# A new order of steps, two row tables on other engines, a split last output chunk and paired ReLUs in a fused attention and FFT-mixing kernel

## The chip, the cores and the metric

The kernel runs on one core of a Trainium2 chip. The core has TensorE (PE in the profile; its weight loads are PEld), VectorE (DVE), ScalarE (ACT), GpSimd (POOL) and SyncE (SP). Each engine takes its instructions in the order in which they were written and waits for others by semaphores. SyncE issues most stores and all transposing transfers here, GpSimd most loads, ScalarE two small ones. The metric is the device time of one execution in microseconds (us), as the median over runs.

## The reference

```python
def phi(x):                                   # x: q or k, (8, 8, 576, 64); w_phi: (64, 128)
    proj = np.einsum('bhsd,df->bhsf', x, w_phi)
    proj = proj - np.max(np.abs(proj), axis=-1, keepdims=True)
    return np.concatenate([np.exp(proj), np.exp(-proj)], axis=-1)
q_p, k_p = phi(q), phi(k)
kv = np.einsum('bhsf,bhsd->bhfd', k_p, v)
z = np.sum(k_p, axis=2)
num = np.einsum('bhsf,bhfd->bhsd', q_p, kv)
den = np.einsum('bhsf,bhf->bhs', q_p, z)[..., None] + 1e-06
x = num / den                                 # heads side by side: (8, 576, 512)

u = x + np.real(fft(fft(x, axis=1), axis=2))  # along the 576 rows, then the 512 columns
un = (u - mean(u)) / sqrt(var(u) + 1e-06)     # over the 512 columns
out = u + np.maximum(un @ w_ch1, 0.0) @ w_ch2 # w_ch1: (512, 2048), w_ch2: (2048, 512)
```

Everything is float32 outside. There are eight batches.

## The kernel before

The work of one batch is cut into streams, each a Python generator, and each `yield` ends a step. A string, `PLAN`, has one letter for each step; `step(name)` runs the next step of that letter's stream, and a stream that has finished goes on with the next batch. So the letters' order is the order in which the instructions of all engines are written, and nothing reorders them later. A step is named here by letter, batch and number, counted from 0: F1.16 is step 16 of the forward stream of batch 1. A place in the plan is counted from 1. The string has 1236 letters before the change.

The streams of one batch:

- K, V, Q load keys, values and queries through GpSimd's queue (L289), cast to bfloat16. B and A transpose the keys and the queries by DMA through SyncE's queue (L413 to L427). The buffers of staged and transposed data are single: the loads of the next batch wait for the transposes of this one.
- T makes the features: step 0 for the last 64 key rows, steps 1 to 8 in pairs for the keys (eight matmuls to `psk`, then two exponentials of 1024 columns, L502), steps 9 to 17 for the queries (L602, L611). R takes the maxima of the keys on VectorE (L511, L516). S scales the values by exponentials of these maxima: small exponentials on ScalarE (L452, L466), multiplications on GpSimd (L456 for the last rows in S.0, L471 for a pair of heads in each of S.1 to S.4). P takes the maxima of the queries (matmuls to `psq`, L560 on VectorE); its last step, P.6, weighs them (a matmul to `pt`).
- M has 26 steps: 0 to 7 build a head's key-value matrix (`kv`, ten matmuls, a copy by ScalarE, L900), 8 to 15 combine it with the queries (L992 on TensorE, L999, L1004 and L1006 on VectorE, L1007 on GpSimd into `X`, with `cb` in two buffers), 16 to 20 are the DFT along the rows, 21 to 25 the DFT along the columns with the additions to `X` (L1099). D, between M.15 and M.16, folds rows and columns of `X` on VectorE (L908 to L932).
- N normalises: for each of five chunks of rows, statistics on VectorE (L1179, L1180), the shift on ScalarE (`UN`, L1155), a transposing DMA from SyncE to `UT` (L1172). The chunks come in the order 0, 2, 1, 3, 4. Batch 0 transposes on TensorE instead. U takes the row scales.
- F, with 68 steps, is the FFN: `hidden(0, 256)` is 16 steps of four matmuls of 256 columns into `psf` (L1224) and one ReLU (L1228) each; then output chunks 0 and 2 (8 steps of two matmuls of 512 columns into `pso` each, L1235, then an addition on VectorE and a store, L1241); `hidden(256, 576)` is 16 steps of 320 columns; then output chunks 1 and 3 and the last chunk of 64 rows (16 matmuls on half the array's columns in turn, L1260; two additions, L1267; a store of 63 rows, L1213, and one of one row, L1214). In batch 0 both hidden parts come first, so the second weight matrix is read from F0.32 on.

`psf`, `pso`, `pu` and, in the first two batches, `psq` share three PSUM banks (`pb`); `psk`, `psh`, `psD` and the combines share `pj`, two buffers of two banks; `kv`, `pt` and the small key tile share one bank (`pk`).

At the start, batch 0's raw inputs are loaded in float32 by SyncE and transposed on TensorE (G for keys, J for queries, copied out by L378 on ScalarE or L380 on VectorE). C builds the tables of angles for the DFT: `at` for rows (three blocks of 320 columns, VectorE), its absolute value `t3` (L220), `tc2` for columns (512, GpSimd), its absolute value `tc3` (L225, VectorE). H takes their sines on ScalarE (L243 to L254). Z clears paddings on GpSimd, Y keeps TensorE busy with matmuls that nothing reads (L1313), and W loads the two weight matrices through GpSimd's queue (L91, L93).

In the plan F steps of one batch stand among the steps that prepare the next ones. From F7.0 (place 1165) only four other steps follow, and the last 47 letters are all F.

## Time and profile before

| | |
|---|---|
| median of 13 runs | 437.08 us (435.97 to 439.26) |
| the profiled execution's own time | 437.75 us |
| its span (first to last instruction) | 436.0 us |
| mean granted TensorE clock | 0.993 |
| TensorE, VectorE, ScalarE, GpSimd busy | 406.2, 334.4, 308.9, 208.6 us |
| first FFN matmul of batch 0 (F0.0) | 54.3 us |
| W1b load, W2b load, issue to landing | 18.2, 15.5 us |
| median landing of a key load of 512 KB | 7.5 us |
| ReLU of 256 and of 320 columns, mean | 388, 444 ns (128 of each) |
| L178 (VectorE, 320 columns), L197 | 1.83 us and 1.91 us for three each |
| L183, L220 (VectorE, 960 columns) | 0.66 us each |
| L225 (VectorE, 512 columns) | 1.65 us |

Times inside the execution are counted from the start of the span. Busy time of TensorE is no measure of how well it is used: its matmuls are pipelined, and a matmul's span holds the time in the pipe. A line of the stretches' view has the stretch, then length, then busy time and number of instructions of PE, PEld, DVE, ACT and POOL, then the granted clock, the mean share of the DMA engines and GB/s. A line of the chain of waits has start, duration, and what the end of the program waited for at that time. A timeline's line has start, duration, engine, line, operation and tiles; SPq is the issuing of transfers by SyncE.

### The profile page before, as it was taken

How to read it: one execution, taken by the hardware profiler on the slowest of the kernel's cores; microseconds unless marked ns; L12 is line 12 of the kernel's file. 1: busy time of each engine (PE TensorE's matmuls, PEld its weight loads, DVE VectorE, ACT ScalarE, POOL GpSimd, SP SyncE). 2: the span in 40 equal slices, each digit the busy share in tenths (PEclk: the TensorE clock that was granted, in tenths of full speed). 3: DMA queues.
4: the chain of work that ended last, by engine and by line, in shares of the span. 5: the costliest groups of instructions: out<-in, count | busy, mean ns of one | idle time of the engine just before them, and what ended most of it. 6: DMA issues, size and time to landing. Idle time of an engine off the chain costs nothing.

```text
span 436.0 us, 10447 instructions
## 1 busy us (share of the span) xinstructions
PE 406.2 (93%) x4110; PEld 255.5 (59%) x4110; DVE 334.4 (77%) x685; ACT 308.9 (71%) x685; POOL 208.6 (48%) x269
## 2 busy tenths in 40 slices
PE   8888798989899999999999899999999999999993
PEld 3565466644675658565766458565766467656551
DVE  6979776799959984998679985898799875965202
ACT  2896899735994798499847798589948885355340
POOL 7982478646645093636645445823642543300100
PEclk9899999999999999999999999999999999999998
DMA  8899994986569366494898446793853150104304
GB/s 218 160 204 150 151 143 50 179 95 100 97 68 144 56 98 118 84 152 58 128 97 120 51 90 101 105 143 63 129 95 51 20 104 20 26 0 86 58 21 84
DMA packets 108626, 42.70 MB, mean 98 GB/s; under 512 B 82849, under 2 KB 103457, under 8 KB 108577
## 3 DMA queue, kind: packets, MB, share of 16 engines
q0 software_dynamic: 45936, 16.60, 35.1%
q1 hardware_dynamic: 62481, 25.38, 30.7%
q8 instruction: 32, 0.52, 0.5%
q14 instruction: 17, 0.14, 0.1%
q10 hardware_dynamic: 160, 0.07, 0.1%
HBM read 36.77 MB, written 9.44 MB: 106 GB/s over the span
## 4 chain that ended last, share of the span: by engine, by line
PE 46%; DVE 34%; ACT 12%; DMA 2%; issue 2%; POOL 2%; DVEq 0%; ACTq 0%; POOLq 0%; SPq 0%
PE psf L1224 17%; PE pso L1235 12%; DVE cb L1004 5%; DVE tg L999 4%; DVE MK L516 4%; DVE R L908 4%; PE kv L892 2%; PE pso L1260 2%; DMA UT<-UN 2%; DVE MQ L560 2%; DVE rd L1006 2%; DVE CEO L1039 2%; ACT HT L1228 2%; DVE X L1241 2%; PE psD L1050 2%
## 5 line engine op out<-in xcount | busy, mean ns | idle before, releaser
L1224 PE MATMUL psf<-UT,W1b 128*128 128x320 bf16 (+1 forms) x1024 | 142.1, 286 | 3.5 <-DMA UT<-UN 2.3
L1235 PE MATMUL pso<-W2b,HT 128*128 128x512 bf16 x512 | 125.7, 379 | 0.0
L1228 ACT ACTIVATE HT<-psf 128x256 bf16<-128x256 f32 (+1 forms) x256 | 100.0, 416 | 34.8 <-PE psf L1224 27.5
L1224 PEld LDWEIGHTS <-W1b 128*128 128x128 bf16 x1024 | 94.6, 98 | 34.9 <-issue 7.5
L1235 PEld LDWEIGHTS <-HT 128*128 128x128 bf16 x512 | 45.8, 98 | 43.9 <-issue 1.3
L1007 POOL TENSOR_TENSOR X<-cb,rd 128x320 f32<-128x320 f32 x56 | 41.1, 734 | 62.0 <-DVE rd L1006 47.3
L471 POOL TENSOR_TENSOR VCn<-VS,VCn 128x512 bf16<-128x512 bf16 x28 | 29.8, 1063 | 35.5 <-ACT VCn L466 29.6
L502 ACT ACTIVATE KPp<-psk 128x1024 bf16<-128x1024 f32 x28 | 28.8, 1029 | 22.3 <-PE psk L496 22.2
L560 DVE TENSOR_REDUCE MQ<-psq 128x8 f32<-128x1024 f32 (+1 forms) x32 | 34.2, 1083 | 10.5 <-PE psq L552 10.4
L1241 DVE SCALAR_TENSOR_TENSOR X<-pso,rs,X 128x512 f32<-128x512 f32 x32 | 23.7, 740 | 23.3 <-PE pso L1235 23.1
L502 ACT ACTIVATE KPn<-psk 128x1024 bf16<-128x1024 f32 x28 | 28.6, 1021 | 13.9 <-DVE MK L516 13.8
L516 DVE TENSOR_REDUCE MK<-psk 128x8 f32<-128x1024 f32 x28 | 34.0, 1213 | 0.3
L1099 DVE TENSOR_TENSOR X<-pu,X 128x512 f32<-128x512 f32 (+3 forms) x49 | 23.5, 528 | 11.8 <-PE pu L1109 11.7
L456 POOL TENSOR_TENSOR V4N<-VS,V4N 64x256 bf16<-64x256 bf16 x14 | 8.9, 637 | 49.0 <-ACT V4N L452 27.6
L1155 ACT ACTIVATE UN<-X,MV 128x512 bf16<-128x512 f32 (+1 forms) x35 | 25.0, 724 | 7.8 <-DVE MV L1180 4.1
L611 ACT ACTIVATE QPHP<-psh 128x1024 bf16<-128x1024 f32 x28 | 28.8, 1027 | 2.2 <-PE psh L602 2.0
L471 POOL TENSOR_TENSOR VCp<-VS,VCp 128x512 bf16<-128x512 bf16 x28 | 29.7, 1060 | 0.0
L611 ACT ACTIVATE QPHN<-psh 128x1024 bf16<-128x1024 f32 x28 | 28.8, 1027 | 0.0
L1179 DVE BATCH_NORM_STATS2 st<-X 128x6 f32<-128x512 f32 (+1 forms) x40 | 26.9, 673 | 0.0
L1195 POOL TENSOR_TENSOR rs<-VE,mhalf 128x5 f32<-128x5 f32 (+1 forms) x9 | 10.3, 1139 | 31.5 <-DVE VE L1194 31.5
L992 PEld LDWEIGHTS <-QPHP 128*128 128x128 bf16 x280 | 20.9, 99 | 5.3 <-DVE cb L1004 1.9
L289 POOL DMA_DIRECT2D QS<-in_q_dram x28 | 23.1, 827 | 0.0
(459 smaller groups left out, 800.1 us busy)
## 6 DMA issues: line engine op xcount, KB each, us to landing
out_dram<-X SPq DMA_DIRECT2D x16, 256.0 KB
out_dram<-X SPq DMA_DIRECT2D x64, 64.0 KB
KS<-in_k_dram POOLq DMA_DIRECT2D x7, 512.0 KB, 7.5
QS<-in_q_dram POOLq DMA_DIRECT2D x14, 256.0 KB, 8.1
VS<-in_v_dram POOLq DMA_DIRECT2D x14, 256.0 KB, 6.3
W1b<-in_moe_w_ch_dram POOLq DMA_DIRECT2D x1, 2048.0 KB, 18.2
W2b<-in_moe_w_ch_dram POOLq DMA_DIRECT2D x1, 2048.0 KB, 15.5
W2b<-in_k_dram SPq DMA_DIRECT2D x2, 512.0 KB
```

Of the source, the lines that this page charges most:

```text
L471: nc.gpsimd.tensor_tensor(out=VC[:, hs, :, 0:D], in0=values[b][0][:, hs, :].rearrange("p h (j d) -> p h j d", d=D), in1=VC[:, hs, :, D:D + ...
L502: nc.scalar.activation(out=KP[:, hs, :, :].rearrange("p e (jp jj) f -> p jj (e jp) f", jj=2), in_=psk[:], func=AT.Exp, scale=sgn,)
L516: nc.vector.tensor_reduce(out=MK[:, 2 * pr:2 * pr + 2, :].rearrange("p e (jp jj) -> p jj (e jp)", jj=2), in_=tiles[pr][:], axis=AX.X, op=A ...
L560: nc.vector.tensor_reduce(out=o, in_=i[:], axis=AX.X, op=ALU.max, apply_absolute_value=True)
L611: nc.scalar.activation(out=o, in_=psh[:], func=AT.Exp, scale=sgn)
L1007: nc.gpsimd.tensor_tensor(out=X[:, :, D * h:D * h + D], in0=cb[:, :, 0:D], in1=rd[:].to_broadcast([128, 5, D]), op=ALU.mult,)
L1155: nc.scalar.activation(out=UN[0:M, c, :], in_=X[0:M, c, 0:C], func=AT.Identity, scale=-1.0, bias=mv[0:M, c, 0:1],)
L1179: nc.vector.bn_stats(out=st[0:M, :], in_=X[0:M, c, 0:C])
L1224: nc.tensor.matmul(ps[:], lhsT=W1b[:, cc, 128 * hh:128 * hh + 128], rhs=UT[:, cc, lo:hi], start=(cc == 0), stop=(cc == NCC - 1),)
L1228: nc.scalar.activation(out=HT[:, hh, lo:hi], in_=ps[:], func=AT.Relu, scale=-1.0)
L1235: nc.tensor.matmul(po[:], lhsT=HT[:, hh, at:at + 128], rhs=W2b[:, hh, :], start=(hh == 0), stop=(hh == NHH - 1),)
L1241: nc.vector.scalar_tensor_tensor(out=U[:, c, 0:C], in0=po[:], scalar=scale_of[b, c], in1=U[:, c, 0:C], op0=ALU.mult, op1=ALU.add,)
```

## The change

- `PLAN` is a new string of 1239 letters. Stream C has six steps and not three. Kinds and numbers of all other steps stay.
- The row angles: the product by the row number moves to ScalarE (three activations with a per-partition scale), the count of whole turns to GpSimd (three operations) and ScalarE (one activation of 960 columns that takes `MAGIC` off), and one VectorE operation of 960 columns joins them. The column angles: the product moves to ScalarE, the rest stays on GpSimd. `magic` is a new constant.
- The last output chunk of batch 7 is computed in two halves of 256 columns, each with its own PSUM tile, additions and stores. The first half's stores go to ScalarE's queue; of the second half the 63 rows go to SyncE's and the one row to ScalarE's.
- In `hidden(0, 256)` two steps share one PSUM tile of 512 columns, and one ReLU takes both after the second.

```diff
--- before.py
+++ after.py
@@ -21,19 +21,19 @@
 
 
 PLAN = (
-    "CYCYZYYZYGTGZKGRTZGTZSGTJKJJRPTTJQRPQYWTSRTSJPTYTMMRTSMMPSTPTPTMMTTMZTPMVMQMTMVVTMDTMBHMDYYDHADYYMHY"
-    "HYMTHMMHMTRWMTNMTSMNYNTMNYNRFFRFNFSFCNFFUTMFNTUNPMFKVFRFQSMTPFTFNTFRSFQSMUFKUVBFTUFMPTPPMTUKFFTQMPFT"
-    "FMTPTFMMTFFFUMFMFATMRKFFFMVFTQDFRTMFFFFFFFMFMFFPTFDFFDSFRFQTFFTMDFFFTFFMFFFFMRFFTFFSMSFMFRPSTMYMTTNF"
-    "QFPTNPPFSMMTMMTMPTMFBFFMTFMFFKFMNFFMFTPFVFFMTNFNUMAFFMTMFFFVMRFTFRFFMFTFFFVMFKFMFMFFTFPFFFRDFTFFDFTP"
-    "FFFFDFDFFQRMTMPFFFFFFMTFSFSMRFMFTFTMTQFNFFTSTMMNFMBSFPPMMFTFFMPTMTFFSFMTQFPFFFMFFMNFFFMTFVMNMFFMFMNF"
-    "UFMFFFMFAFFMTFMFKVFTFFFRFRFMFTFFVQKTPFRFFFDTFFFTDFFFDQFFFDRMFFTMTFSFFMFSMRFFTFMFTPFMFFSTTMNFFNMFFTFT"
-    "NFMFFFMMSTPMSFTQFMFFPPTBMFFFMNKFMNFFMFVTPFMFFPUMFFMFAMFFMTFRFMFFMFFFVMTFRFKFTFMFVFFFQDQTPFFFFRFDTFFT"
-    "PFFFDDFFFRMTFFFTFFFMSMMFSRFTMFTFTMFMTFTNNMFMFMFMTFSFMTPSMFTNFFFPPPSFFMFFFFBMFFMTFFMFVFPTQFFMNNUMAFVF"
-    "FMFTMFKTFRFFRSFFMTFFFFMMKFFFTVFMFFQFRPFTQFDFFMTRFDFFFFFFFDFTDFFMFFFMTFMFSMFMFFRTTMFTMFFTNFTNFSMFTMMM"
-    "TFNSFPMFTFSFMPQFFMFTPPBMFFMTPFFMFPNFFVMAFNUMMFFTFMFMFFMFFFFTRVPFRFTFFFMFFFMFTVFFRMFFDDFTFFFTPFFFFFDF"
-    "FDFRTMTFMFFFFMMFSSFMRFTFMTFTTFMNFFFNSMTFMMSFMFTTFTNFFPMFSFPPTFMFFFMFFFMFNPMFFMFFPNFFFMMFFFTUMMFFFFFM"
-    "FMFFFMFMFFFFMFFDDFFFFFFDFFDFMMFFFFMFFMMFFFMFMNNFMFFFFFFFFNFFMFFFFFFFFFFFFFFFMFFNFNFFFFFFUFFFFFFFFFFF"
-    "FFFFFFFFFFFFFFFFFFFFFFFFFFFFFFFFFFFF"
+    "YYCCYCYGCGZTGRTGZTZTZRZJQQGSTJRKTPYTSTPRYTWJJJRMPTMTSSMTPPSTPTMTZQMTMMTMPMMVKBTCMTMDTYMVHMYYDYYDDAHM"
+    "HYYHTHMMMHKMTTRMNMTMYQNNYVMSNTKNMFFNFNRRFSTPFTPTUFWMNFFMNFFSFRTFVMFFTCURPSYUBNTUTFSUFMFQKTFMFTPPMQTP"
+    "VMTFFPUTFUMTMFFAFMMTFFMQFMFDFRFMFTVFFFFRFMFTFFMFFPFFTFFFQDDFFFRFMFTKFFDMTFFFFTFMFFMFRTFMRTFMFSSSSTTM"
+    "NPFFTNPBTMMMSMQFTMTPPMFFMFFTMFFFPVTAMFFFPNFFMTFFMNNKUMFFVMMFFQTMFFTFRMRFFTFFFQFMFFMFMFFFPTFFRFFFFDFD"
+    "VFTPFFFDFFDKTPRFTFFMMTSFFBFFFMMSSFFMFFRTMTMFFTNMSMFFFTNPPMFMTFFFTMTFSTPMFFFMFFQPFTFMFFVFNMFFFMKTFFAM"
+    "NNMFFMFUMFVFFMVQFFMFTTRFFMFFFKFRFFMTQFFFDTMRFFFFFDTPFFFTDDFRPFFFFFMTFTFMFFMFBMRFSSMFFTTTMFMTFFFTFNFN"
+    "SFMTTMMFFFPMFTMSTPPMFFSMTFFMNFPFMFFPFFVKMNQKFFMNMUFFMFFMFFVMFAFMFQMFFMFTTRFQRFFFTVFMFFFFDFTPFRFFFPDT"
+    "FFFTFFFDFFFDRTMTMFFFFMBFSMFFSMRFTFTTMSFMFTFNMMMTMFTFFFMNFPSSTMTNFFFFTPPMFFFMFTFPQMFVFKFPFFMFFMANMFFN"
+    "FFMKFFMFTUTFMFFRFRFFSVFMFFFFFTMFTFQFRMFDVTFFFMTRFFDFFFFFFFDFFDFTMFTBQFMFFMSFMFRFMFTFTTMFFSMTNFTNFFMP"
+    "SMFFMMTFMPTFSMTFFMTPFMFTFFQMFNPPPFVMFFAMFFPFNNUMVFMFTFMFMFFFMFRFFMTRTFSFFFFFPFFMFVFMTFFRFFTFDFDFPTFF"
+    "FFDDFRFFTTMMFFFFFFMMFRSFTFFMTFTMTFFNTFSMNFFFMTFTTFMFMFMTSPFMFFFFMFFSMFTPPMFFFMFFMNPFMFFPNNFUMMFFFFMF"
+    "FMFFFMMFFFFFFMFFMFFFDFFDFFFDFFDFMFFFFMMFMFMFFFMNMFNFFFFFFFFMMFFFFFFFFFFFFFFFFFFFFNMNFNFFFFFUFFFFFFFF"
+    "FFFFFFFFFFFFFFFFFFFFFFFFFFFFFFFFFFFFFFF"
 )
 
 
@@ -78,6 +78,8 @@
 
     halfpi = const.tile([128, 1], F32, name="halfpi")
     nc.vector.memset(halfpi[:], float(np.pi / 2))
+    magic = const.tile([128, 1], F32, name="magic")
+    nc.vector.memset(magic[:], -MAGIC)
     ones_b = const.tile([128, 128], BF16, name="ones_b")
     nc.vector.memset(ones_b[:], 1.0)
 
@@ -173,34 +175,9 @@
         nc.vector.tensor_copy(out=ident_b[:], in_=ident[:])
         count(tn[:, 1, :], [[1, 128]], 0, 1)
 
-    def angles(eng, out, turns, idx, period, cols):
-        for j, at_ in enumerate(cols):
-            eng.tensor_scalar(
-                out=turns[:, at_], in0=idx, scalar1=pn[:, j:j + 1] if len(cols) > 1 else pn[:, 3:4],
-                scalar2=MAGIC, op0=ALU.mult, op1=ALU.add,
-            )
-        whole = slice(cols[0].start, cols[-1].stop)
-        eng.tensor_scalar(
-            out=turns[:, whole], in0=turns[:, whole], scalar1=MAGIC, scalar2=-float(period),
-            op0=ALU.subtract, op1=ALU.mult,
-        )
-        for j, at_ in enumerate(cols):
-            k_ = j if len(cols) > 1 else 3
-            if eng is nc.gpsimd:
-                eng.tensor_scalar(
-                    out=out[:, at_], in0=idx, scalar1=pc[:, k_:k_ + 1], scalar2=None, op0=ALU.mult
-                )
-                eng.tensor_tensor(
-                    out=out[:, at_], in0=out[:, at_], in1=turns[:, at_], op=ALU.add
-                )
-            else:
-                eng.scalar_tensor_tensor(
-                    out=out[:, at_], in0=idx, scalar=pc[:, k_:k_ + 1], in1=turns[:, at_],
-                    op0=ALU.mult, op1=ALU.add,
-                )
-
     at, t3 = gs[:, 0:3 * NK], ga[:, 0:3 * NK]
     tc2, tc3 = ga[:, 1280:1280 + C], ga[:, 1792:1792 + C]
+    turns, turns_c = gs[:, 1024:1024 + 3 * NK], gc[:, C:2 * C]
 
     def constants(b):
         nc.vector.tensor_single_scalar(
@@ -213,15 +190,33 @@
         )
         nc.vector.tensor_scalar_mul(out=pn[:, 0:3], in0=pc[:, 0:3], scalar1=1.0 / S)
         nc.vector.tensor_scalar_mul(out=pn[:, 3:4], in0=pc[:, 3:4], scalar1=1.0 / C)
-        angles(
-            nc.vector, at, gs[:, 1024:1024 + 3 * NK], rs, S,
-            [slice(NK * j, NK * j + NK) for j in range(3)],
-        )
+        for j in range(3):
+            nc.scalar.activation(
+                out=t3[:, NK * j:NK * j + NK], in_=rs, func=AT.Identity, scale=pc[:, j:j + 1]
+            )
+            nc.gpsimd.tensor_scalar(
+                out=turns[:, NK * j:NK * j + NK], in0=rs, scalar1=pn[:, j:j + 1], scalar2=MAGIC,
+                op0=ALU.mult, op1=ALU.add,
+            )
+        yield
+        nc.scalar.activation(out=turns, in_=turns, func=AT.Identity, bias=magic[:])
+        nc.vector.scalar_tensor_tensor(
+            out=at, in0=turns, scalar=-float(S), in1=t3, op0=ALU.mult, op1=ALU.add
+        )
+        yield
         nc.vector.tensor_single_scalar(
             out=t3.bitcast(I32), in_=at.bitcast(I32), scalar=0x7FFFFFFF, op=ALU.bitwise_and
         )
         yield
-        angles(nc.gpsimd, tc2, gc[:, C:2 * C], rc, C, [slice(0, C)])
+        nc.scalar.activation(out=tc2, in_=rc, func=AT.Identity, scale=pc[:, 3:4])
+        nc.gpsimd.tensor_scalar(
+            out=turns_c, in0=rc, scalar1=pn[:, 3:4], scalar2=MAGIC, op0=ALU.mult, op1=ALU.add
+        )
+        nc.gpsimd.tensor_scalar(
+            out=turns_c, in0=turns_c, scalar1=MAGIC, scalar2=-float(C), op0=ALU.subtract, op1=ALU.mult
+        )
+        nc.gpsimd.tensor_tensor(out=tc2, in0=tc2, in1=turns_c, op=ALU.add)
+        yield
         nc.vector.tensor_single_scalar(
             out=tc3.bitcast(I32), in_=tc2.bitcast(I32), scalar=0x7FFFFFFF, op=ALU.bitwise_and
         )
@@ -1218,14 +1213,23 @@
         HT = fpool.tile([128, NHH, S], BF16, tag="HT", name="HT")
 
         def hidden(lo, hi):
+            two = hi - lo == 256
             for hh in range(NHH):
-                ps = pb.tile([128, hi - lo], F32, tag="pb", name="psf")
+                if not two or hh % 2 == 0:
+                    psw = pb.tile([128, 512 if two else hi - lo], F32, tag="pb", name="psf")
+                ps = psw[:, 256 * (hh % 2):256 * (hh % 2) + 256] if two else psw[:]
                 for cc in range(NCC):
                     nc.tensor.matmul(
-                        ps[:], lhsT=W1b[:, cc, 128 * hh:128 * hh + 128], rhs=UT[:, cc, lo:hi],
+                        ps, lhsT=W1b[:, cc, 128 * hh:128 * hh + 128], rhs=UT[:, cc, lo:hi],
                         start=(cc == 0), stop=(cc == NCC - 1),
                     )
-                nc.scalar.activation(out=HT[:, hh, lo:hi], in_=ps[:], func=AT.Relu, scale=-1.0)
+                if not two:
+                    nc.scalar.activation(out=HT[:, hh, lo:hi], in_=ps, func=AT.Relu, scale=-1.0)
+                elif hh % 2:
+                    nc.scalar.activation(
+                        out=HT[:, hh - 1:hh + 1, lo:hi], in_=psw[:].rearrange("p (a n) -> p a n", a=2),
+                        func=AT.Relu, scale=-1.0,
+                    )
                 yield
 
         def output(c):
@@ -1254,6 +1258,28 @@
             yield from hidden(256, S)
         yield from output(1)
         yield from output(3)
+        if b == B - 1:
+            for at in (0, 256):
+                po = pb.tile([128, 256], F32, tag="pb", name="pso")
+                for hh in range(NHH):
+                    g = 64 * (hh % 2)
+                    nc.tensor.matmul(
+                        po[g:g + 64, :], lhsT=HT[:, hh, 512:576], rhs=W2b[:, hh, at:at + 256],
+                        start=(hh < 2), stop=(hh >= NHH - 2),
+                    )
+                    if hh == 7:
+                        yield
+                for g in (0, 64):
+                    nc.vector.scalar_tensor_tensor(
+                        out=U[0:64, 4, at:at + 256], in0=po[g:g + 64, :],
+                        scalar=scale_of[b, 4][0:64], in1=U[0:64, 4, at:at + 256],
+                        op0=ALU.mult, op1=ALU.add,
+                    )
+                queue = nc.sync if at else nc.scalar
+                queue.dma_start(out=out[b, 257:320, at:at + 256], in_=U[1:64, 4, at:at + 256])
+                nc.scalar.dma_start(out=out[b, 0:1, at:at + 256], in_=U[0:1, 4, at:at + 256])
+                yield
+            return
         po = pb.tile([128, C], F32, tag="pb", name="pso")
         for hh in range(NHH):
             g = 64 * (hh % 2)
@@ -1324,7 +1350,7 @@
         "U": (scales, 1), "P": (part(0), 7), "T": (part(1), 18), "R": (part(2), 5),
         "S": (part(3), 5), "K": (fetch_k, 2), "V": (fetch_v, 3), "Q": (fetch_q, 3),
         "A": (arrive, 1), "B": (arrive_k, 1), "W": (load_ffn_weights, 2),
-        "C": (constants, 3), "H": (sines, 6), "Y": (stir, 16), "G": (turn_first_k, 5), "J": (turn_first_q, 5), "Z": (pads, 6),
+        "C": (constants, 6), "H": (sines, 6), "Y": (stir, 16), "G": (turn_first_k, 5), "J": (turn_first_q, 5), "Z": (pads, 6),
     }
     LONGER = {("N", 0): 10, ("U", 0): 7, ("M", 0): 24, ("T", 0): 20}
     at_ = {name: (1 if name in "KVBQA" else 0, 0) for name in STREAMS}
```

## The prediction

> **What bounds the kernel now.** I read the page first, then busy time by stretches of 20 us, then the chain of waits, then timelines of the two ends. Steps are named as in the section on the kernel: F1.16 is step 16 of the forward stream of batch 1.
>
> ```profile
> PE 406.2 (93%) x4110; PEld 255.5 (59%) x4110; DVE 334.4 (77%) x685; ACT 308.9 (71%) x685; POOL 208.6 (48%) x269
> 40.00:60.00 20.00, 15.70 (x130) 9.45 (x129) 15.98 (x48) 17.16 (x39) 8.69 (x14) 1.00 1.24 162
> 60.00:80.00 20.00, 18.42 (x243) 13.17 (x243) 13.70 (x30) 19.93 (x47) 15.15 (x19) 1.00 0.77 83
> 80.00:100.00 20.00, 18.23 (x174) 9.76 (x173) 19.17 (x40) 10.64 (x20) 11.89 (x14) 1.00 0.92 118
> ```
>
> TensorE looks like the bound, but no engine is it everywhere: ScalarE fills 60 to 80 (19.93 of 20), VectorE 80 to 100 (19.17). After 120 TensorE is at 18.5 to 20 per 20 us.
>
> How much of TensorE's time is waiting? From its timeline I took the spacing from the first matmul of each plan step to that of the next, less the tenth percentile of that spacing for the same kind: 0.43 us for an FFN step of 256 columns, 0.54 for 320, 0.43 for two output matmuls, 0.32 for a head's key-value step, 0.31 for a combine, 0.75 and 1.12 for the DFT steps M18 and M20. From F0.0 (54.3 us) to the last F step the excess is 31.5 us: 10.3 between 60 and 120, some 20 in the other 300 us. So after 54.3 no order can win more than about 31 us; before 54.3 TensorE waits for latencies.
>
> The chain of waits at the start, and at a handover to the next batch's FFN:
>
> ```profile
> 8.87 1.66 POOL ga L193
> 10.55 1.65 DVE ga L225
> 12.20 0.03 issue
> 12.23 0.69 DVE KT L380
> ...
> 206.11 1.63 PE pso L1260 x13
> 207.73 3.06 DMA UT<-UN
> 210.80 0.14 issue
> 210.93 1.03 PE psf L1224 x8
> ```
>
> VectorE's second key copy (L380) stands behind the column table (L225), which waits for GpSimd. At 210.93 TensorE has used up its other work and waits for the transposed UT. The same excess stands at F2.0 (1.02), F3.0 (1.12), F4.0 (0.53) and F6.0 (1.04): 3.7 us.
>
> The tail, from the timeline (start, duration):
>
> ```profile
> 424.37 5.10 SPq L1205 DMA_DIRECT2D out_dram<-X  x8
> 426.86 1.92 PE L1260 MATMUL pso<-W2b,HT 128*64 128x512 bf16 x16
> 428.89 1.53 DVE L1267 SCALAR_TENSOR_TENSOR X<-pso,rs,X 64x512 f32<-64x512 f32 x2 [1.10 <-PE pso L1260]
> 429.58 0.65 SPq L1211 DMA_DIRECT2D out_dram<-X  x1
> 430.45 0.31 SPq L1213 DMA_DIRECT2D out_dram<-X  x1
> 430.82 0.27 SPq L1214 DMA_DIRECT2D out_dram<-X  x1
> ```
>
> SyncE is issuing other stores until 430.23. From the last issue's end (431.09) to the end of the span (436.0) are 4.9 us.
>
> **What the Trainium skill says.** "ScalarE: Activation LUTs", *What ACT_TABLE_LOAD costs*: an activation takes 186 ns + 0.833 ns per column, each per-partition pointer operand 93 ns more, and neighbours overlap by 93. The trace agrees: 388 ns for 256 columns (399 by the page), 0.27 us apart in a chain of three. "SBUF — State Buffer", *SBUF: two separate sides*: VectorE's two-port operations and GpSimd lock each other out. Agrees: L220 takes 659 ns for 960 columns, L225 1646 ns for 512 beside GpSimd. "DMA: Bandwidth & Descriptors", *Issuing engines are not separate DMA queues*: a second issuing engine saves issue time alone; that is all I count for the tail.
>
> **The change part by part.** Sums are against the profiled execution, 437.75 us (span 436.0 and 1.75 around it); it lies 0.67 over the median of 437.08.
>
> *Tail.* The 16 matmuls (1.92 us) become twice 16 of half the width: 2 x 0.94, so TensorE still ends at 428.8. The first half's two VectorE additions hide behind the second half's matmuls. The second half's are 256 wide: by L1030 (65x257, 473 ns) about 0.43 apart, so VectorE ends at 429.75 and not 430.42 (-0.67). But SyncE is free only at 430.23: the last large store goes out at about 430.35 to 430.66, row 0 meanwhile from ScalarE, which is idle here. Last issue 430.66 against 431.09: **-0.4** (0 to -0.7; nothing if the landing, not the issue, sets the end).
>
> *Row tables.* VectorE loses three multiplies (1.83), L183 (0.66) and three fused operations (1.91): 4.4 us. It gains one of 960 columns (1.06 by rate, 1.91 if as slow as L197's three). ScalarE gains four operations of 320, 320, 320 and 960 columns with pointers: 3 x 0.45 + 0.99 = 2.3 us (estimate by the ScalarE page), hidden in its wait for w_phi and the first keys (idle 3.45 to 5.92 and 3.19 us before 9.41), and one of 512, 0.61 us, behind the first key copy at 9.78, not hidden. GpSimd gains three of 320 columns, about 0.6 each, and its memsets come later. L225 goes from before the key copies to place 80, where it costs VectorE 0.3 to 1.65 in a stretch with gaps of 0.3 to 0.5. The key copy then waits only for its transposes, at about 11.3 and not 12.23: 0.9 earlier; the first V4N exponentials, for which ScalarE stops at 14.16 to 15.10, come later too. Against it stand the 0.61. To F0.0 I take **-1.0** (-2 to +1).
>
> *Paired ReLUs.* 64 pairs at 2 x 0.27 become 64 of 512 columns at 0.49 (K4n at 46.91, same size): 0.05 each. It counts where ScalarE is full, batch 0's eight pairs, and on the 12% of the chain that is ScalarE: 0.4 + 56 x 0.05 x 0.12 = 0.7. A pair holds one PSUM bank across two steps, but three banks then cover six; against a bank held half full beside the psq pairs I take **-0.4** (-1 to +0.5).
>
> *Order, handovers.* TensorE work between M22 (X complete for the chunk of N1) and F0, from the steps' spacings, batches 2, 3, 4, 6: 6.24, 6.23, 8.03, 6.66 before; 7.75, 7.97, 8.71, 5.28 after. By that the 3.7 becomes about 2.4. Between N1 and F0 it is 5.81, 5.37, 7.38, 5.37 before and 4.95, 5.60, 4.21, 5.28 after: 3.9 less in sum, all of it a loss if VectorE runs up to N1 no earlier. I take **-0.8** (-3.7 to +2.5).
>
> *Order, batch 2's values.* S2.0 to S2.3 now stand in a row, with 2.8 us of TensorE work before M2.0 (15.0 before). GpSimd needs 4 x 0.65 for S2.0 and 2.1 for S2.1: 4.7 us. VectorE work holds TensorE there too (N1.0, P2.1, M1.22: 2.7), so **+1.0** (0 to +2).
>
> *Order, batch 1's weighing.* P1.6 waits 0.99 us at 75.52 for the PSUM slot that M1.6 holds; two F steps now stand between them: **-0.9** (-0.99 to 0).
>
> *Order, the rest.* 31.5 - 3.7 - 0.99 = 26.8 us of excess in many small waits. Speaking for less: work between the last query exponentials (T17) and M8 grows in batches 4 to 7 from 2.16, 1.17, 3.76 and -1.60 us to 6.10, 4.93, 5.92 and 6.23; key loads no longer follow the transposes that free their buffer (GpSimd waits 5.6 us for that). Speaking for more: Q6.0 stands 4 places behind A5.0 (32 before), so GpSimd can wait for those transposes with batch 4's combines (L1007) queued behind it, VectorE behind those by the two cb buffers. I take 7%, **-2.0** (-8 to +4); a choice, not a derivation.
>
> *Moved loads.* W's second load goes from place 112 to 151, issued near 60 instead of 46.8; at 15.5 us it lands near 76, before F0.32 (84.6): nothing, unless it needs over 23 us. K1.1 is the rival below.
>
> Sum: -0.4 - 1.0 - 0.4 - 0.8 + 1.0 - 0.9 - 2.0 = -4.5: 433.25, and with the 0.67 **432.6** against the median.
>
> **Rivals.** *Nothing from the order* (0.20): waits move but their sum stays, because VectorE's 334 us and ScalarE's 309 must still interleave with TensorE's. Then tail and pairs alone remain: 436.3. For it: the distances at most other edges differ by under 1 us between the orders. That the tail does not shorten, since the store's landing sets the end, is the same case with 0.4 more.
>
> *A larger gain* (0.13): a third of the 31.5 goes, and 1 at the start: 437.08 - 11.5, with half of the other losses, near 427.5. For it: the longer distances above. Against: the handovers are still short.
>
> *Batch 1's keys come late* (0.17, slower). K1.1 goes from place 26 to 77: GpSimd issued it at 17.1, now at about 33.4, in a queue with W1b (18.2 us to land from 19.8). With 7.5 us it lands at 41; two transposes at the loaded pace seen at 24.73 (10.87 for both) give the first half near 48, and T1.1 needs it at 49.0. Each us beyond that is a us, for TensorE is in order and ScalarE full from 49.4 on. From 5.4 us late the gain is gone; with keys landing 8 us later than that, 440.5. Against it: W1b has landed by 40, and unloaded transposes take 1.6 each.
>
> **How the numbers follow.** The likeliest case has 0.50: 432.6, its own range 430.0 to 435.5. A measurement tells from no change what exceeds 0.2%, 0.9 us: 436.2 to 438.0 is "same". Faster: 0.50 + 0.13 + 0.12 of the first rival = 0.75; same: 0.06 of it and 0.02 of the slow one; slower: 0.02 + 0.15 = 0.17. The range of 8 in 10 leaves out half of the large gain and most of the slow case: 428.5 to 438.5.
>
> **What would show it.** First F matmul near 53.3; VectorE's first key copy before 11.5; the ReLU row of 512 columns x64 at some 610 ns; no wait of PE for UT<-UN over 1 us in batches 2 and 3; a V4N wait near M2.0; last issue 0.4 after SyncE's previous one. Wrong it is if psk of batch 1 waits for KT, or if the excess between F0.0 and the end is 31 or more.

## The result, and the profile after

The changed kernel takes 427.55 us (median of 11 runs, 426.76 to 429.78); the kernel before, on the same chip, 437.12 (48 runs). The ratio is 0.9785, with a 95% interval of 0.9766 to 0.9804: 9.6 us less, where 4.5 were forecast. The time lies just below the forecast range. The profiled execution took 427.41 us and its span is 425.6 (436.0 before).

The page's line of busy time, and two of the stretches that were shown of before (start and end of the stretch, length, then PE, PEld, DVE, ACT, POOL, clock, DMA share, GB/s):

```profile
PE 403.1 (95%) x4126; PEld 255.3 (60%) x4126; DVE 332.0 (78%) x682; ACT 305.3 (72%) x626; POOL 207.1 (49%) x271
60.00:80.00 20.00, 19.58 (x261) 14.22 (x259) 15.64 (x35) 19.22 (x43) 15.09 (x18) 1.00 1.37 162
80.00:100.00 20.00, 19.31 (x152) 9.49 (x150) 19.45 (x41) 10.06 (x15) 7.06 (x9) 1.00 1.10 123
```

No engine lost much busy time: VectorE 2.4 us, ScalarE 3.6, TensorE 3.1. TensorE is fuller from 60 to 100 (38.9 us of 40, 36.65 before). Over the whole span it is busy 3.1 us less and idle 7.3 us less (22.5 and not 29.8), so most of the 10.4 us between the spans went from waiting.

A handover is where TensorE goes on to the next batch's FFN, which needs the transposed UT. Two handovers of the chain of waits, F3.0 and F4.0, whose transfers stood at 207.73 and 257.22 before (start, duration, what the end waited for):

```profile
204.83 2.43 DMA UT<-UN
207.31 1.05 PE psf L1222 x8
...
250.83 3.69 DMA UT<-UN
```

F3.0 still waits, but for 0.47 us and not 1.12. F4.0 waits longer, 0.82 us and not 0.53. F2.0 and F6.0 hardly wait.

Where the 10.4 us between the two spans went, from TensorE's timelines, by the prediction's measure (the excess is the spacing of steps less the tenth percentile of their kind):

| | before | after | difference |
|---|---|---|---|
| F0.0 starts | 54.35 | 52.02 | -2.3 |
| excess from F0.0 to the last F step | 31.4 | 24.6 | -6.8 |
| of it handovers F2.0, F3.0, F4.0, F6.0 | 3.7 | 1.3 | -2.4 |
| spacings inside the work of those steps (remainder) | | | -0.5 |
| end of TensorE to end of span | 7.19 | 6.40 | -0.8 |

By size, 13 waits of 0.5 us or more held 11.4 us before; now 9 hold 7.6. Those from 0.2 to 0.5 fell from 6.0 to 4.5, those below 0.2 from 13.9 to 12.6.

The two ends, from the timeline (start, duration, engine, line, operation, tiles):

```profile
1.11 5.72 PE L1339 MATMUL idle<-ones_b 128*128 128x512 bf16 x16 [1.11 <-DVE keep L130]
6.77 0.46 PE L368 MATMUL pst<-ident,HT 64*128 64x64 f32 x4
9.21 0.69 DVE L375 CAST KT<-pst 128x512 bf16<-128x512 f32 x1
...
417.29 1.94 PE L1266 MATMUL pso<-W2b,HT 128*64 128x256 bf16 x32
418.47 2.02 DVE L1273 SCALAR_TENSOR_TENSOR X<-pso,rs,X 64x256 f32<-64x256 f32 x4 [0.25 <-PE pso L1266]
...
420.10 0.66 ACTq L1280 DMA_DIRECT2D out_dram<-X  x2
421.43 0.31 SPq L1279 DMA_DIRECT2D out_dram<-X  x1
```

VectorE's first key copy is at 9.21 and not 12.23. The first key transposes begin at 6.77. Ahead of them stand 16 idle matmuls. Before there were 20, and the transposes began 2.1 us later:

```profile
1.09 7.89 PE L1313 MATMUL idle<-ones_b 128*128 128x512 bf16 x20 [1.09 <-DVE keep L128]
8.91 0.46 PE L373 MATMUL pst<-ident,HT 64*128 64x64 f32 x4
```

At the tail the last issue ends 2.5 us after TensorE's end, 2.3 before: later, not earlier. What shrank is the time from that issue to the end of the span, 4.9 to 3.9 us.

### The profile page after: what moved, and what is told of

The parts are those of the page before. It is cut to its first block, busy times and chain, and to the rows that moved or that the text cites. A ratio compares the mean times of both kernels' runs of the same rounds, so it can differ in the third digit from the quotient of the medians.

```text
span 425.6 us, 10430 instructions
## 1 busy us (share of the span) xinstructions
PE 403.1 (95%) x4126; PEld 255.3 (60%) x4126; DVE 332.0 (78%) x682; ACT 305.3 (72%) x626; POOL 207.1 (49%) x271
## 4 chain that ended last, share of the span: by engine, by line
PE 47%; DVE 33%; ACT 13%; issue 2%; POOL 2%; DMA 1%; DVEq 0%; ACTq 0%; POOLq 0%
PE psf L1222 16%; PE pso L1239 14%; DVE cb L999 5%; DVE R L903 4%; DVE MK L511 4%; DVE tg L994 4%; PE kv L887 3%; PE pso L1286 2%; DVE CEO L1034 2%; PE pu L1104 2%; DVE MQ L555 2%; ACT KPn L497 2%; DVE rd L1001 2%; DVE X L1245 2%; PE psD L1045 2%
## 5 line engine op out<-in xcount | busy, mean ns | idle before, releaser
L1227 ACT ACTIVATE HT<-psf 128x320 bf16<-128x320 f32 x128 | 53.5, 451 | 24.8 <-PE psf L1222 19.3
L1229 ACT ACTIVATE HT<-psf 128x512 bf16<-128x512 f32 x64 | 38.4, 599 | 14.3 <-PE psf L1222 14.0
L555 DVE TENSOR_REDUCE MQ<-psq 128x8 f32<-128x1024 f32 (+1 forms) x32 | 34.2, 1085 | 14.8 <-PE psq L547 14.5
L451 POOL TENSOR_TENSOR V4N<-VS,V4N 64x256 bf16<-64x256 bf16 x14 | 8.8, 630 | 53.2 <-ACT V4N L447 48.3
## 6 DMA issues: line engine op xcount, KB each, us to landing
W2b<-in_moe_w_ch_dram POOLq DMA_DIRECT2D x1, 2048.0 KB, 17.7
```

Source lines behind the costliest of these rows:

```text
L555: nc.vector.tensor_reduce(out=o, in_=i[:], axis=AX.X, op=ALU.max, apply_absolute_value=True)
L1227: nc.scalar.activation(out=HT[:, hh, lo:hi], in_=ps, func=AT.Relu, scale=-1.0)
L1229: nc.scalar.activation(out=HT[:, hh - 1:hh + 1, lo:hi], in_=psw[:].rearrange("p (a n) -> p a n", a=2), func=AT.Relu, scale=-1.0,)
```

## The experiments

Steps are written out in place of letters; all ratios are to the kernel before. Two theories stood at the outset: the gain is the sum of small code and order gains at named places (the prediction), or it is the order as such, with waits that can't be told apart.

### Code or order

Four kernels: the tail alone; the paired ReLUs alone; the new plan on the old code; all new code with the old order (C's three letters spread over its six steps).

```diff
 # tail alone: before, with the new branch for b == B - 1
 # pairs alone: before, with the new hidden(lo, hi)
 # order alone: before, PLAN = the new string
+    "C": (constants, 6)   # the old table operations, cut in six steps
 # code alone: after, PLAN = the old string
-... C0 ... C1 ... C2 ...
+... C0 C1 C2 ... C3 C4 ... C5 ...
```

> The kernel before with the split last output chunk alone; plan, tables and ReLUs as before. The theory of the prediction (the last store's issue sets the end) expects -0.4 us, so 436.7, and the last issue by SyncE earlier than before relative to TensorE's last matmul. The trace of the changed kernel has the last issue no earlier (2.5 us after the end of TensorE's work, 2.3 before) but the end 0.8 us nearer to it; the rival, that the amount still queued on one queue sets the end, expects -0.8, so 436.3, with the last issue in place. If neither holds: 437.1.

> The kernel before with the paired ReLUs alone. By rate (0.05 us a pair where ScalarE is full) -0.4 us: 436.7. The rival, that pairs also free ScalarE and PSUM for what TensorE waits for, expects -1.5 or more: 435.6 or less. A loss (437.5 or more) if the bank that a half-finished pair holds makes the psq pairs wait.

> The new order alone: the tables stay on VectorE and GpSimd as before (only cut into the six steps that the new plan has letters for), single ReLUs, the last chunk whole. If the order is the change's substance: about 429.5, that is 7.5 us under before, with the first transposes of keys near 6.8 us and FFN step F0.0 near 52.5. If the code changes carry it, or if the order only pays together with paired ReLUs: 433 or more.

> All code changes with the order of before (the letters C tripled, doubled and single, so that each of the old three steps becomes its new parts in place). If the order is the change's substance: 435.5 (tail 0.8, pairs 0.4, tables 0.3 since five idle-matmul steps still stand ahead of the first key transposes). If the code carries it: 431 or less.

| kernel | median us | ratio | interval |
|---|---|---|---|
| tail alone | 437.05 | 0.9985 | 0.9970 to 1.0001 |
| pairs alone | 437.54 | 1.0009 | 0.9994 to 1.0024 |
| order alone | 428.99 | 0.9812 | 0.9780 to 0.9843 |
| code alone | 436.11 | 0.9971 | 0.9955 to 0.9988 |

The order is 8 of the 9.6 us; all code together is 1.3. The pairs alone show no gain. The tail alone does not stand clear of the noise in its median, but in the traces: TensorE's end is 6.34 to 6.44 us from the span's end in all 13 kernels with the split chunk, and 6.83 to 7.28 in the 7 without it. Its last issue is 2.45 us after TensorE's end, as in after.

### The start and the rest, apart

Both orders have F0.0, so the first part of one can be joined to the second part of the other there: steps that the first part has done are struck from the second, and steps it lacks are caught up at the joint.

```diff
 # new start: all new code
+new order up to F0.0, then the old order
 # old start: all new code
+old order up to F0.0, then the new order
 # fifth idle step behind, in before
-Y0.3 Z0.1 Y0.4 G0.0 T0.0
+Y0.3 Z0.1 G0.0 Y0.4 T0.0
 # fifth idle step ahead, in after
-Y0.3 G0.0
+Y0.3 Y0.4 G0.0
```

> All code changes; the new order up to F0.0 and the order of before for everything after it. If the start (F0.0 2.3 us earlier) and the rest add up: 437.1 - 2.3 - 0.8 (tail) - 0.4 (pairs) = 433.6. If the steady part takes the start's gain back: 435.9. If the steady part's gain came from the start: 428.

> The reverse: all code changes, the order of before up to F0.0 and the new order after it. If start and rest add up: 427.6 + 2.0 = 429.6, with the excess of TensorE's spacing after F0.0 near 25 us (31.4 before, 24.6 in the changed kernel). If the new order's steady part needs its own start: 432 or more.

> The kernel before with one letter moved: the fifth step of idle matmuls (4 matmuls that nothing reads) goes behind the first key transposes. In the trace of before TensorE runs 20 idle matmuls until 8.9 us and only then the transposes, though the last key rows seem to have landed by 5.8; in the changed kernel it is 16 until 6.8. Theory: idle matmuls ahead of the transposes hold the start; the transposes then begin near 7.0 and the median falls by 0.3 to 1.5 us (not by 2.1, for the second key copy still waits on VectorE for the column table until 12.2). Rival (my prediction's reading: the landing of the keys holds them): transposes stay near 8.9, median 437.1.

> The changed kernel with the same letter moved the other way: a fifth step of idle matmuls ahead of the first key transposes. If these matmuls hold the start: transposes near 8.9, F0.0 near 53.5 to 54, time 1 to 2 us above the changed kernel (428.6 to 429.6). If the landing of the keys decides: no change, 427.6.

| kernel | median us | ratio | interval |
|---|---|---|---|
| new start, old rest | 436.22 | 0.9970 | 0.9953 to 0.9986 |
| old start, new rest | 430.03 | 0.9821 | 0.9791 to 0.9851 |
| before, idle step behind | 438.18 | 1.0015 | 0.9998 to 1.0032 |
| after, idle step ahead | 429.57 | 0.9812 | 0.9787 to 0.9836 |

The part after F0.0 makes about 6 us of the order's gain by itself (430.03 against 436.11). The start's share is less clear: taking the new start away from after costs 2.5 us, giving it to the old order brings nothing. In after, an idle step ahead of the key transposes moves them from 6.77 to 9.10 and F0.0 from 52.02 to 53.65; in before, the same four matmuls taken away move them only from 8.91 to 8.00, and F0.0 comes later, at 55.75. Order alone, with the old table operations, has F0.0 at 52.01: the new table code is not what moved it.

What blurs this is TensorE's granted clock. Most profiles have an early stretch at half clock, 3.41 or 6.83 us long, and it lies elsewhere each time: 17.0 to 20.4 us in before, 14.5 to 17.9 in after, 17.5 to 24.3 in before with the idle step moved, 23.2 to 30.0 with new start, old rest. Of the eight kernels here with the new order up to F0.0, the three with 3.41 us of it near 14.6 have F0.0 at 52.0; the other five, four of them with 6.83 us, have it at 53.8 to 54.2. Six kernels with the old order have 3.41 us of it near 16.6, and F0.0 at 54.0 to 54.6. With the same length of early half clock, then, the new start brings F0.0 about 2 us forward, but its traces more often have the longer one.

The medians contain such differences of the clock, too. Of the runs of before beside the first four kernels, the 24 with a granted clock of 0.996 or more have a median of 436.45 us, the 14 with 0.990 or less 438.84. Code alone had a mean clock of 0.995 over its runs, new start with old rest 0.992. Of the runs at 0.993 and 0.994 alone, code alone has 436.7 us (9 runs), new start with old rest 435.2 (7 runs): 1.5 us that the two medians do not show.

### Does the gain belong to places?

The same joint, moved to F2.0 and to F4.0, both ways round, all with the new code.

```diff
+new order up to F2.0, then old        # and its complement: old up to F2.0, then new
+new order up to F4.0, then old        # and its complement: old up to F4.0, then new
```

> All code changes, new order up to F2.0, old order from there (ends of the scale: 436.1 us with the old order throughout, 427.6 with the new). Gains add up by place (theory): at F2.0 the traces of the two kernels stand 5.1 us apart, about 4.5 of it from the order, so 431.6. The new order pays only as a whole, as at F0.0 (rival): the old part waits for what it waited for before, 435 to 436.

> All code changes, old order up to F2.0, new order from there: the complement of the first run. Gains add up by place: the gains of the two over 436.1 make 8.5 together, so 432 if the first is 431.6. As a whole only: the two gains together fall well short of 8.5.

> All code changes, new order up to F4.0, old from there. Gains add up by place: the traces stand 6.6 us apart at F4.0, about 6 of it from the order, so 430. As a whole only: 433 or more.

> All code changes, old order up to F4.0, new order from there: the complement of the second run. Gains add up by place: 433.5, batches 4 to 7 alone. As a whole only: 435 or more, and with the second run's gain well short of 8.5.

| kernel | median us | ratio | interval |
|---|---|---|---|
| new to F2.0, then old | 433.45 | 0.9913 | 0.9886 to 0.9940 |
| old to F2.0, then new | 431.05 | 0.9853 | 0.9804 to 0.9902 |
| new to F4.0, then old | 432.78 | 0.9893 | 0.9837 to 0.9949 |
| old to F4.0, then new | 436.72 | 0.9964 | 0.9945 to 0.9983 |

Against code alone (0.9971), the pair at F2.0 gains 0.58% and 1.18%: 1.76% together, where the whole order gains 1.86%. So the gains add up by place, within the intervals. The pair at F4.0 gives 0.78% and 0.07%, less than half; by its times alone it speaks for the rival, that the order pays only as a whole. The lengths from one Fx.0 to the next, from the traces, show another cause (us; the order of each stretch in brackets, o old, n new):

| kernel | F0-F1 | F1-F2 | F2-F3 | F3-F4 | F4-F5 | F5-F6 | F6-F7 |
|---|---|---|---|---|---|---|---|
| before | 61.7 o | 48.1 o | 46.7 o | 50.3 o | 45.4 o | 48.1 o | 41.9 o |
| code alone | 61.7 o | 47.6 o | 47.0 o | 50.6 o | 45.4 o | 48.3 o | 41.5 o |
| after | 59.3 n | 47.8 n | 48.2 n | 47.3 n | 44.9 n | 46.6 n | 41.2 n |
| old start, new rest | 59.4 n | 47.8 n | 48.7 n | 47.0 n | 44.9 n | 46.6 n | 41.2 n |
| new to F2.0, then old | 59.3 n | 47.9 n | 48.0 o | 50.5 o | 45.4 o | 48.3 o | 41.5 o |
| old to F2.0, then new | 61.7 o | 47.7 o | 48.4 n | 46.6 n | 44.9 n | 46.6 n | 41.2 n |
| new to F4.0, then old | 59.3 n | 47.8 n | 48.4 n | 48.9 n | 46.3 o | 48.3 o | 41.5 o |
| old to F4.0, then new | 60.7 o | 48.8 o | 46.9 o | 53.0 o | 44.5 n | 46.6 n | 41.2 n |

Away from the joints a stretch has nearly the same length in every kernel that has its order, whatever the others have. (The largest exception: old to F4.0 has 1 us less from F0 to F1, behind a half clock just ahead of F0.0, and 1 us more from F1 to F2.) The gain sits in three: F0 to F1 (-2.4 us), F3 to F4 (-3.0 to -3.7) and F5 to F6 (-1.5); F2 to F3 gives back 1.5. Part of this is only work that changes its stretch. By the steps' usual spacings, 0.8 of the 1.5 is three more steps of TensorE between F2 and F3; F0 to F1 has 0.7 us of work less, F3 to F4 some 0.5, F5 to F6 0.3. In F5 to F6 another 0.9 is the handover F6.0.

The joints cost time of their own. At F2.0 it is 0.95 us: M3.2 is caught up right ahead of F2.0, and M3.3 then waits for ScalarE's copy, so the old stretch behind it takes 48.0 and not 47.0. The cut at F4.0 goes through a gaining stretch, and the steps caught up ahead of F4.0 lengthen it: 53.0 and 48.9. In new to F4.0 a half clock from 258.66 to 262.07 follows, and F4 to F5 takes 46.3 and not 45.4. In old to F4.0 all steps keep their spacing to before within 0.15 us from F3.0 on until that joint; there T5.16, caught up ahead of F4.0, waits for VectorE's query maxima:

```profile
262.69 2.36 DVE L555 TENSOR_REDUCE MQ<-psq 128x8 f32<-128x1024 f32 x2
263.97 0.39 PE L597 MATMUL psh<-QT,wphi 64*128 64x512 bf16 x2 [2.33 <-DVE MQ L555]
264.62 0.60 PE L1222 MATMUL psf<-UT,W1b 128*128 128x256 bf16 x4
```

### Which edges? One step moved at a time

In F3 to F4 of before, five waits of 0.47 to 0.98 us hold 3.3 us; after has two, of 0.23 and 0.82. The largest pair is at M4.20 and T5.9 (0.86 and 0.98). There VectorE's column fold for M4.20 runs beside GpSimd's values S5.0:

```profile
245.96 1.51 POOL L456 TENSOR_TENSOR V4N<-VS,V4N 64x256 bf16<-64x256 bf16 x2 [9.54 <-ACT V4N L452]
245.97 1.92 DVE L1039 TENSOR_TENSOR CEO<-R 128x381 bf16<-128x381 f32 x2
...
247.94 1.06 PE L1050 MATMUL psD<-CS,CEO 128*128 128x289 bf16 x6 [0.70 <-DVE CEO L1039]
```

The Trainium skill, "SBUF — State Buffer", *SBUF: two separate sides*, says that a GpSimd operation that reads SBUF and a VectorE operation with two inputs in SBUF take turns on a shared pair of ports. The trace agrees: VectorE's pair takes 1.92 us here, and 1.02 in the two kernels below, where GpSimd does nothing meanwhile. After has this pair at 240.02, and GpSimd begins at 241.14. Two kernels move S5.0 in before, the first by much, the second by two places. (The new order has it one place earlier, between M4.18 and M4.19, not behind M4.19 as the expectation of the second says.)

```diff
-... M4.17 S5.0 M4.18 M4.19 F3.53 S5.1 R5.4 F3.54 T5.8 M4.20 F3.55 ...
+... M4.17 M4.18 M4.19 F3.53 R5.4 F3.54 T5.8 M4.20 S5.0 S5.1 F3.55 ...   # S5 far
+... M4.17 M4.18 M4.19 S5.0 F3.53 S5.1 R5.4 F3.54 T5.8 M4.20 F3.55 ...   # S5 near
```

> The kernel before with two letters moved: S5.0 and S5.1 go from ahead of M4.19 and F3.54 to behind M4.20. In the trace of before GpSimd's multiplications of S5.0 (245.96 to 249.0) run beside VectorE's two CEO operations of M4.19, which take 1.92 us for both (1.03 elsewhere), and TensorE waits 0.86 us at M4.20. Theory (the two engines shut each other out, and where S stands beside M.19 decides): CEO at 1.03, the wait at M4.20 under 0.2; the median falls by 0.5 to 0.9 us if the saving reaches the end, and stays at 437.1 if the next wait takes it. Rival (something else slows CEO): wait unchanged.

> Before, with one letter moved: S5.0 stands behind M4.19 and not ahead of M4.18, as in the new order, so its exponentials follow the cast of the first row transform on ScalarE. GpSimd then begins at about 247.3 and not 245.96, when VectorE's pair at the column fold (245.97, 1.92 us for two) is over. If the stretch from F3.0 to F4.0 is longer in the old order for this collision (theory): M4.20 and T5.9 lose 1.3 of their 1.84 us of waits as when S5 went behind M4.20, the values are only 1.4 us later and not 4.1, so M5.0 waits little: 49.1 to 49.7 us for the stretch of 50.3, the total 0.6 to 1.2 us less, ratio near 0.998. If waits removed singly always come back (rival): 50.1 or more, ratio 1.000.

S5 far: 437.59 us, 1.0001 (0.9984 to 1.0018), F3 to F4 50.2. S5 near: 436.27 us, 0.9968 (0.9951 to 0.9985), F3 to F4 49.1 against 50.3: one letter is worth 1.2 us there, of the 3.0 to 3.7 that the whole order gains in this stretch. The rest of them was not taken apart. Timeline of S5 far, and then of S5 near:

```profile
245.55 1.02 DVE L1039 TENSOR_TENSOR CEO<-R 128x381 bf16<-128x381 f32 x2
...
250.03 1.31 POOL L456 TENSOR_TENSOR V4N<-VS,V4N 64x256 bf16<-64x256 bf16 x2 [14.03 <-ACT V4N L452]
...
254.92 0.29 PE L892 MATMUL kv<-VCp,KPp 128*128 128x65 bf16 x4 [1.16 <-POOL VCp L471]
```

```profile
245.30 1.02 DVE L1039 TENSOR_TENSOR CEO<-R 128x381 bf16<-128x381 f32 x2
246.74 1.31 POOL L456 TENSOR_TENSOR V4N<-VS,V4N 64x256 bf16<-64x256 bf16 x2 [10.98 <-ACT V4N L452]
...
253.40 0.29 PE L892 MATMUL kv<-VCp,KPp 128*128 128x65 bf16 x4
```

Both remove the collision and bring T5.9 1.3 us forward (counted from F3.0). S5 far starts GpSimd 4.5 us later (counted likewise), and M5.0 then waits 1.16 us for the values: the gain is paid back. S5 near starts it 1.5 us later, and M5.0 waits for nothing.

Four more moves, two at the places of the prediction's steps and two in after:

```diff
 # P1.6 later, in before
-M1.6 T1.15 P1.6 T1.16 F0.22 M1.7
+M1.6 T1.15 T1.16 F0.22 P1.6 M1.7
 # S2 spread, in after
-F0.46 ... F0.55 ... F0.60 ... F0.64 S2.0 S2.1 S2.2 S2.3 T2.9 T2.10
+F0.46 S2.0 ... F0.55 S2.1 ... F0.60 S2.2 ... F0.64 S2.3 T2.9 T2.10
 # S2.2 and S2.3 behind T2.10, in after
-S2.0 S2.1 S2.2 S2.3 T2.9 T2.10
+S2.0 S2.1 T2.9 T2.10 S2.2 S2.3
 # S3 later, in after
-T3.7 S3.0 F1.49 ... M2.19 S3.1 S3.2 F1.54 F1.55 M2.20 F1.56 F1.57
+T3.7 F1.49 ... M2.19 F1.54 F1.55 M2.20 S3.0 S3.1 F1.56 S3.2 F1.57
```

> The kernel before with one letter moved: P1.6 goes behind F0.22, so that T1.16 and an FFN step of 0.54 us stand between it and M1.6, for whose PSUM slot it waited 0.99 us. The prediction counted such a wait in full: 0.8 us less, 436.3. Rival: ScalarE is full here until 76 us, so the wait moves to the next step that needs ScalarE; 437.1.

> The changed kernel with S2.0, S2.1 and S2.2 no longer in a row with S2.3: they go behind F0.46, F0.55 and F0.60. In the trace the eight small exponentials of the row (103.04 to 104.4) stand ahead of T2.9's on ScalarE, and TensorE waits 1.78 us at T2.11. If this row is that wait's cause and the saving reaches the end: about -1.0 us, 426.5. If VectorE, full from 80 to 100, pays instead for GpSimd's multiplications that now run there: 427.6 or more.

> After, with S2.2 and S2.3 moved behind T2.10. Of the eight small exponentials ahead of T2.9 and T2.10 on ScalarE, the four for the first heads stay (S2.0, S2.1), the others follow the feature exponentials. S2.1 makes the exponentials of two pairs, so S2.2 and S2.3 may bring ScalarE little: T2.11's wait of 1.78 us at 106.4 falls by 0.5 to 1.1 and the stretch from F0.0 to F1.0 from 59.3 to 58.3 to 58.8, the total by 0.5 to 1, ratio 0.976 to 0.977 (theory: ScalarE's order sets this wait). If the wait is set by something else (TensorE's psh slots or the query maxima on VectorE): 59.3 and 0.9785.

> The changed kernel with S3.0 to S3.2 moved behind M2.20: there S3.0's multiplications (146.03 to 149.1) run beside the CEO operations of M2.19 (1.91 us for two) and TensorE waits 1.02 us at M2.20. Theory: CEO at 1.03, the wait gone, 0.5 to 1.0 us less: 426.6 to 427.1. Rival: the wait moves on, 427.6.

*P1.6 later*: 439.51 us, 1.0051 (1.0032 to 1.0069), slower. P1.6 no longer waits, but M1.7 does: its `kv` and P1.6's `pt` share a bank, and `pt` is now read late. The timeline, and the two stretches around it:

```profile
76.66 0.29 PE L892 MATMUL kv<-VCp,KPp 128*128 128x65 bf16 x4 [1.74 <-ACT E L575]
```

```profile
73.96:77.37 3.41, 1.67 (x29) 1.36 (x28) 0.00 (x0) 2.84 (x9) 1.72 (x3) 1.00 1.22 156
77.37:80.78 3.41, 3.41 (x22) 2.06 (x19) 1.24 (x4) 2.01 (x5) 1.87 (x2) 0.50 1.74 147
```

M1.7 starts 0.9 us later than in before, counted from F0.0. Then the clock is halved for 3.41 us, right behind 3.41 us in which TensorE was busy for 1.67, and F0.26 starts 2.6 us later. So the wait that moved accounts for some 0.9 us, and the half clock for 1.7. That the wait brought the half clock on is likely and not shown; the mean clock of this kernel's runs is 0.990, that of the runs of before beside them 0.994.

*S2 spread*: 434.66 us, 0.9929 (0.9905 to 0.9954), 7 us slower than after. Of the 7.9 us between the two spans 2.0 lie ahead of F0.0, where the half clock is 6.83 us long and not 3.41, and 1.6 between F1 and F2. F0 to F1 itself grew from 59.3 to 63.8. GpSimd's multiplications now lie in VectorE's fullest stretch, and the column folds meet them twice:

```profile
98.42 1.88 DVE L1034 TENSOR_TENSOR CEO<-R 128x384 bf16<-128x384 f32 x2
98.62 1.26 POOL L466 TENSOR_TENSOR VCn<-VS,VCn 128x512 bf16<-128x512 bf16 x1 [1.03 <-issue]
99.85 1.36 POOL L466 TENSOR_TENSOR VCp<-VS,VCp 128x512 bf16<-128x512 bf16 x1
101.60 2.37 DVE L1034 TENSOR_TENSOR CEO<-R 128x381 bf16<-128x381 f32 x2
```

In after both pairs take 1.02 us. The two pairs lost 2.2 us. On TensorE the 4.5 us show as a longer wait at M1.20 (2.3 us, 0.7 in after), two of 0.8 at M1.16 and F0.59, and 2.3 at the handover F1.0, where after waits for nothing; T2.11's wait falls from 1.8 to 1.0. Around F1.0 the clock is halved once more:

```profile
115.06:118.47 3.41, 1.28 (x25) 1.01 (x19) 2.42 (x3) 0.98 (x2) 0.15 (x1) 1.00 1.42 174
118.47:121.88 3.41, 3.41 (x34) 2.72 (x32) 0.00 (x0) 1.35 (x4) 0.69 (x1) 0.50 1.03 160
```

That is the 1.6 us between F1 and F2. Against these three places the row of S2 steps is the better one; the places that before had were not tried in after.

*S2.2 and S2.3 behind T2.10*: 429.08 us, 0.9798 (0.9770 to 0.9826), no different from after. The wait aimed at is the largest left in after; the small exponentials of S2 stand ahead of T2.9's on ScalarE:

```profile
103.04 0.44 ACT L447 ACTIVATE V4N<-MK 64x4 bf16<-64x4 f32 x2
103.51 0.46 ACT L447 ACTIVATE V4P<-MK 64x4 bf16<-64x4 f32 x2
104.44 1.00 ACT L606 ACTIVATE QPHP<-psh 128x1024 bf16<-128x1024 f32 x1
...
106.40 0.39 PE L597 MATMUL psh<-QT,wphi 64*128 64x512 bf16 x2 [1.61 <-ACT QPHN L606]
```

S2.2 has no exponentials of its own (S2.1 makes those of two pairs, S2.3 the next), so only two of the eight moved, 0.20 us. T2.11 came 0.20 earlier (its wait 1.57 and not 1.78), and M2.0's wait for the values rose from 0.28 to 0.48. M2.0 starts where it did, at 108.24.

*S3 later*: 428.20 us, 0.9786 (0.9757 to 0.9816), no different from after. But its place gained. The new order has a collision of its own, between S3.0 and the column fold of M2.19. Here is the fold's second pair in after, and then in S3 later:

```profile
146.04 1.91 DVE L1034 TENSOR_TENSOR CEO<-R 128x381 bf16<-128x381 f32 x2
```

```profile
147.50 1.02 DVE L1034 TENSOR_TENSOR CEO<-R 128x381 bf16<-128x381 f32 x2
```

The wait of 1.02 us at M2.20 is gone, and F1 to F2 takes 47.1 and not 47.8. The medians of 6 and 11 runs can't show 0.7 us.

No kernel here is faster than after by more than the noise.

## Why the prediction was right and wrong

Direction and place were right: it is the order and TensorE's waits, not work. The number was off by a factor of two: in the spans 10.4 us went and not 4.5. The three terms that were too small are the rest of the order (by 2.4), the handovers (1.6) and the start (1.3). Step by step:

- **"Order, the rest" (-2.0) is the step that failed.** Between F0.0 and the last F step 6.8 us went; without handovers (-2.4), P1.6's wait (-1.0) and the wait that came at T2.11 (+1.0), 4.4 remain for this step, 16% of its 26.8 us and not 7%. The idea of many small waits was right: without the waits that had terms of their own, those of 0.5 us or more went from 5.9 to 5.0 us, those from 0.2 to 0.5 from 6.0 to 4.0, those below 0.2 from 13.9 to 12.5. The share of 7% was a choice that nothing was worked out for, and it was too small. Two of the larger waits have a cause that one moved letter shows, GpSimd beside VectorE: the old order lost 1.2 us to it at M4.19, the new one loses 0.7 at M2.19, where before had none. The prediction did not set VectorE and GpSimd side by side in the steady part, though it had seen the effect at L225. What shortened the many small waits stays open.
- **"Order, handovers" (-0.8): right sign, measured -2.4.** In sum the distances from M22 to F0 (-1.3) were a better guide than those from N1, but not one by one: at F4.0 they left no wait, and it is 0.82 us; at F6.0 they had it grow, and it is gone. What VectorE and the transposes did in between was not taken apart.
- **"Batch 2's values" (+1.0): the size came by luck, at another engine.** M2.0 waits 0.28 us for GpSimd's values; the price is T2.11's wait, 1.78 us against 0.77, behind ScalarE's exponentials of S2. Two of these behind T2.10 took 0.20 off it.
- **"Batch 1's weighing" (-0.9): the wait is gone, the gain is not.** New waits of 0.58 (M1.5) and 0.39 us (M1.6) stand beside it, and the same step moved alone in before made the kernel 0.5% slower. The prediction asked only whether P1.6 would wait, not who waits for its bank.
- **"Row tables" (-1.0 to F0.0): measured -2.3, by another cause.** L225 did hold VectorE's key copy, by some 1.0 us: the transposes for it ended at 11.26, L225 at 12.20. But the first transposes stood behind 20 idle matmuls of some 0.4 us, 16 now, and the prediction never counted the Y steps ahead of G. The new table code with the old order has F0.0 at 54.19, 0.16 us earlier than before; the old table code with the new order has it at 52.01. How much of the -2.3 is real in the median stays open: 0 to 2.5 us by the medians, some 2 where the early half clock is alike.
- **"Tail" (-0.4): size about right (-0.4 to -0.9 in the traces, tail alone 0.9970 to 1.0001), reason wrong.** The last issue is not earlier after TensorE's end; its store lands sooner. Whether that is the smaller store or the second queue was not tried.
- **"Paired ReLUs" (-0.4): nothing to be seen** (pairs alone 0.9994 to 1.0024), though 64 ReLUs of 512 columns took 599 ns as foreseen (some 610). That ScalarE's time is not what TensorE waits for there is the likely reason, and was not traced.
- **"Moved loads" (0): right.** W2b took 17.7 us to land, and F0.32 at 82.26 waits for nothing. The slow rival is out too: T1.1 starts at 46.19, 48.17 before.
- **The rival "a larger gain" (427.5, chance 0.13) is what came,** with a smaller share of the waits than it assumed (22%, not a third), and 2.3 and 0.8 us at the ends. That its number was met to 0.1 us is luck. Its "against", that the handovers stay short, was the wrong part.

## What to carry to other kernels

When a plan for several in-order engines changes, compare stretches between fixed points, not single waits: here a stretch away from the joints mostly kept its length to some 0.8 us, whatever stood around it, while a removed wait was a gain only where the next reader of the moved step did not come to wait in its turn. Look at the granted clock of each stretch first: a half clock of 3.41 us added 1.6 us to a stretch here, more than most moves were worth. Before a step is moved, look on both sides: who waits for it later, which bank it holds, and what VectorE does while GpSimd is at its work. A wait with two suppliers (T2.11 and M2.0 on ScalarE's and GpSimd's order) only changed hands when one of them was served first.
